# Banded attention and an MLP on one core: the scores of the third and fourth batches as 64 by 64 quarters of the TensorE array

## The chip, the core and the metric

The kernel runs on one core of one Trainium2 chip. The metric is device time in microseconds (us): the median of several runs of the whole program. One execution is also recorded by the hardware profiler; its instructions, waits and transfers are the profile that this document reads.

Engine names follow the profile: PE is TensorE's matmuls, PEld its weight loads, DVE is VectorE, ACT is ScalarE, POOL is GpSimd, SP is the engine whose queue issues all transfers. PSUM, into which PE writes, has eight banks.

## What is computed

Four batches of eight attention heads, each over 768 queries of 64 numbers, then for every batch a small mixing over tokens and a two-layer MLP. Cut to what matters here:

```python
B, H, S, D = 4, 8, 768, 64           # block = 32, window = 16, nb = 24
k_sum = k.reshape(B, H, nb, 32, D).max(axis=3)
v_sum = v.reshape(B, H, nb, 32, D).mean(axis=3)
scores_l = scale * q @ k.T            # kept where |i - j| < 16
scores_s = scale * q @ k_sum.T + log(32)
a = softmax(concat([scores_l, scores_s], axis=-1))
x = a @ concat([v, v_sum], axis=2)    # heads side by side: 768 x 512 per batch
u = x + (x.T @ U @ V).T
out = u + relu(u @ w_ch1) @ w_ch2     # 512 -> 2048 -> 512
```

## The kernel before

**Scores.** A head's 768 queries make six tiles of 128. A tile holds two groups of 64 queries, and each group sees its own 96 neighbouring keys and the 24 block maxima: 120 columns (`KC`). Both halves of the 128 partitions carry numbers of the 64 head dimensions: partitions 0 to 63 of the key tile `kt` hold the window of one group of 64 queries, partitions 64 to 127 that of the other. The query tile `qz` is laid out so that each group of 64 queries stands in its own half of the partitions, and zeros, written once at the start, stand in the other half. One matmul of 128 by 128 queries against 128 by 120 keys (line 321, `scores`) thus gives both groups their own keys: the zeros cancel the wrong half. Half of the array multiplies by zero. The work is in float32, and each such matmul shows in the trace as two weight loads and two matmuls (LDWEIGHTS and MATMUL). `scores(st, h, a)` does tiles 3a to 3a+2 into one PSUM bank, and `exponentials(st, h, a)` reads that bank: DVE adds the mask and takes the row's minimum (line 341), ACT takes the exponential (line 351).

**After the scores.** `turn_squares` (line 371) transposes blocks of 32 on DVE, a trip through memory (lines 376 and 384) turns the rest, `square_values` (line 423) multiplies with the values in 24 matmuls of 32 array columns each (`tile_position=(0, 32*i)`), and `normalise` (lines 435 to 437) divides. `mix_t` (line 537) and `mix_s` (line 555) begin the token mixing; `mix_rows` (line 601) and `operands` (lines 610, 184, 185, 636 to 648) finish it and make the operands of the MLP's first layer.

**The order of the work.** It is written by hand: each engine runs its instructions strictly in the order in which the program lists them. The first batch's attention runs alone. The attention of batches 2, 3 and 4 is cut into 32 steps per batch (`later_step`), with seven pieces of mixing put between them at a place that `MIX` sets and seven after them (`later_steps`), and these steps are spread between the matmuls of the MLP of the batch before (line 1185 onwards). For the third and fourth batches the first 15 steps (heads 0 to 4) fall in the MLP's first layer (line 1066, `up_phase`), the rest (heads 5 to 7 and the mixing) in its second (line 1151, `down_phase`). Step 3h does `scores(h, 0)` with its exponentials, step 3h+1 `scores(h, 1)` with its exponentials, step 3h+2 `square_values(h-2)`, `normalise(h-2)` and `turn_squares(h)`.

**Banks and weights.** All PSUM tiles share the eight banks. In `down_phase` six of them hold the accumulators `acc`, so that everything else takes turns in two. At the start of each of its 16 rounds (18 matmuls) `gates` has ACT (line 1135) and DVE (line 1136) make the left operands `gh` and `gl` of the next round. Weights come back from memory in `whole` (line 748), are rounded by ACT (line 184) and the rest taken by POOL (line 185).

Of the kernel before, what the change touches and what calls it, by code (L numbers as in the profile page):

```python
# [10 lines left out]
F32 = mybir.dt.float32  # L11
# [7 lines left out]
P = 128  # L19
BLOCK, WIN = 32, 16  # L20
NB = S // BLOCK
NU = S // P
W = 64 + 2 * WIN
KC = NB + W
# [4 lines left out]
ORDER = (1, 2, 3, 4, 5, 0)  # L29
KP = 2 * W + NB  # L30
# [54 lines left out]
def body(ctx: ExitStack, tc, q0, q1, k, v, vn, uv, w1, w2, mask, ident, rep, out):  # L85
    nc = tc.nc
# [4 lines left out]
    small = ctx.enter_context(tc.tile_pool(name="small", bufs=2))  # L91
# [5 lines left out]
    def bank(name):  # L97
        return psum.tile([P, 512], F32, name=name, tag="bank")
# [116 lines left out]
    def load_qk(st, h):  # L215
        load_k(st, h)
        load_q(st, h)
# [7 lines left out]
    def load_v(st, h):  # L225
        vt = kv.tile([KC, 2, NU, DV], F32, name="vt")
        nc.sync.dma_start(out=vt[:W, 0], in_=v[st.b, 0, :, h])
        nc.sync.dma_start(out=vt[NB:, 1], in_=v[st.b, 1, :, h])
        st.vt[h] = [vt[:, i] for i in range(2)]
# [7 lines left out]
    def load_vsum(st, g, i):  # L237

        parts = 1 if st.b == 0 else 2
        n = BLOCK * D // (2 * parts)  # L240
        spare = None
        if st.b == 1 or st.b == 2 and g == 0:
            spare = hidden_place(2 + i)
        st.vn[g, i] = []
        for j in range(parts):
            if st.b == 0:
                t = vn0[g, i]
            elif spare is not None:
                t = spare[:, j * n : (j + 1) * n]
            else:  # L250
                t = mo.tile([P, DM], F32, name="stage", tag="val", bufs=VALS)[:, :n]
            k = i * parts + j
            nc.sync.dma_start(out=t, in_=vn[st.b, g, :, k * n : (k + 1) * n])
            st.vn[g, i].append(t)
# [22 lines left out]
    def key_maxima(st, h):  # L277
        block_maxima(st, h)
        spread_maxima(st, h, nc.vector.tensor_copy)
# [25 lines left out]
    def value_summaries(st, h, i, copy):  # L305
        r0, r = 32 * (h % 4), (W, 0)[i]
        copy(
            st.vt[h][i][r : r + NB],
            st.vsum[h // 4][r0 : r0 + NB].unsqueeze(1).broadcast_to([NB, NU, DV]),
        )  # L310

    def scores(st, h, a):
        if h not in st.neg:
            st.neg[h] = small.tile([P, NU], F32, name="neg")
        qt, kt = st.qt[h].rearrange("p u q -> p (u q)"), st.kt[h]
        ps = bank("ps_s")
        for i in range(3):
            u = 3 * a + i
            j = ORDER.index(u)
            k0 = (j // 2) * KP + (j % 2) * KC  # L320
            nc.tensor.matmul(  # L321
                ps[:, i * KC : (i + 1) * KC],
                qt[:, 64 + j * P : 64 + j * P + P],
                kt[:, k0 : k0 + KC],
                start=True,
                stop=True,
            )
        st.ps_s[h, a] = ps

    def exponentials(st, h, a):  # L330
        ps = st.ps_s.pop((h, a))
        if h not in st.e and st.b == 0:
            st.e[h] = e0[h % 4]
        elif h not in st.e:
            st.e[h] = att.tile([P, NU * KC + PAD], F32, name="e", bufs=1)
            nc.gpsimd.memset(st.e[h][:, NU * KC :], 0.0)
        e = tiles_of(st.e[h])[:, 3 * a : 3 * a + 3]
        for i in range(3):
            u = 3 * a + i
            m = 0 if u == 0 else (3 if u == NU - 1 else 1 + u % 2)  # L340
            nc.vector.tensor_tensor_reduce(  # L341
                out=e[:, i, :],
                in0=ps[:, i * KC : (i + 1) * KC],
                in1=mask_sb[:, m, :],
                scale=-SCALE,
                scalar=BIG,
                op0=ALU.add,
                op1=ALU.min,
                accum_out=st.neg[h][:, u : u + 1],
            )  # L350
            nc.scalar.activation(  # L351
                e[:, i, :],
                e[:, i, :],
                AF.Exp,
                bias=st.neg[h][:, u : u + 1],
                scale=-1.0,
            )

    def tiles_of(e):
        return e[:, : NU * KC].rearrange("p (u k) -> p u k", k=KC)  # L360

    def turn_squares(st, h):

        e = st.e.pop(h)
        squares = att.tile([P, 4, NU, 32], F32, name="squares", bufs=1)

        src = bass.AP(tensor=e.tensor, offset=e.offset, ap=[e.ap[0], [32, 4], [KC, NU], [1, 32]])  # L370
        nc.vector.transpose(squares, src)
        st.at[h] = squares

    def send_squares(st, h):
        there = dram.tile([P, 4, NU * 32], F32, name="there")
        nc.sync.dma_start(out=there, in_=st.at[h].rearrange("p j u q -> p j (u q)"))
        st.at[h] = there

    def fetch_squares(st, h):

        there = st.at[h].rearrange("(i k) j c -> j k i c", k=32)
        at = st.at[h] = att.tile([P, 4, NU, 32], F32, name="at", bufs=1)
        for j in range(4):
            nc.sync.dma_start(
                out=at[32 * j : 32 * j + 32].rearrange("k i u q -> k i (u q)"), in_=there[j]
            )
# [30 lines left out]
    def square_values(st, h):  # L417

        at, vt = st.at.pop(h), st.vt[h]
        ps = st.psx[h] = bank("ps_x")  # L420
        for u in range(NU):
            for i in range(4):
                nc.tensor.matmul(  # L423
                    ps[32 * i : 32 * i + 32, u * DV : (u + 1) * DV],
                    at[:KC, i, u],
                    vt[u % 2][:, (u // 2) * 2 + (i // 2 + u) % 2],
                    start=True,
                    stop=True,
                    tile_position=(0, 32 * i),
                )  # L430

    def normalise(st, h):
        ps = st.psx.pop(h)[:, : NU * DV].rearrange("p (u d) -> p u d", d=DV)
        s = small.tile([P, NU], F32, name="sum")
        nc.vector.tensor_scalar_add(s, ps[:, :, D], 1e-9)
        nc.vector.reciprocal(s, s)
        nc.vector.tensor_tensor(
            st.x[:, :, h * D : (h + 1) * D],
            ps[:, :, :D],
            s.unsqueeze(2).broadcast_to([P, NU, D]),  # L440
            ALU.mult,
        )
# [25 lines left out]
            slow.pop(0)  # L468

    STEPS = 32  # L470
    MIX = (18, 30)

    def later_step(st, i):

        h, a = divmod(i, 3)
        if a == 0:
            if 1 <= h <= H:  # L480
                send_squares(st, h - 1)
            if 2 <= h <= H + 1:
                fetch_squares(st, h - 2)
            if h < H:
                scores(st, h, 0)
                exponentials(st, h, 0)
            if 3 <= h <= H:
                load_v(st, h - 1)
        elif a == 1:
            if h < H:  # L490
                scores(st, h, 1)
                exponentials(st, h, 1)
            if h + 1 < H:
                key_maxima(st, h + 1)
            if 1 <= h <= H:
                for t in range(2):
                    value_summaries(st, h - 1, t, nc.scalar.copy)
        else:
            if h + 2 < H:
                load_qk(st, h + 2)  # L500
            if h == 2:
                st.x = mo.tile([P, NU, DM], F32, name="x")
            if 2 <= h <= H + 1:
                square_values(st, h - 2)
                normalise(st, h - 2)
            if h < H:
                turn_squares(st, h)
        if st.b > 1:
            if i in (2, 5):
                load_vsum(st, 1, i // 5)  # L510
            if i in (4, 7):
                slow.append(add_vsum(st, 1, i // 7))
        if i in MIX:
            c = 2 * MIX.index(i)
            mix_t(st, c, 2)
            mix_t_out(st, c, 2)
        if i - 1 in MIX:
            c = 2 * MIX.index(i - 1)
            mix_s(st, c, 2)
            mix_s_out(st, c, 2)  # L520

    def later_steps(st):

        todo = [(later_step, st, i) for i in range(STEPS)]
        between = [(mix_rows, st, 0, k) for k in range(3)] + [(operands, st, 0, k) for k in range(4)]
        for n, x in enumerate(between):
            todo.insert(MIX[0] + 3 + 2 * n, x)
        return todo + [(mix_rows, st, 1, k) for k in range(3)] + [(operands, st, 1, k) for k in range(4)]


# [315 lines left out]
    st = sts[0]  # L846
# [98 lines left out]
    for word in START.split():  # L945
        name = word.rstrip("0123456789.")
# [238 lines left out]
    for b in range(1, B):  # L1185
        cur, ahead, after = ([*sts, None, None][b + i] for i in range(3))
        todo = later_steps(ahead) if ahead else []
# [120 lines left out]
```

## Time and profile before

| | |
|---|---|
| median of 3 runs | 678.85 us (678.16 to 680.5) |
| profiled execution | 678.02 us, of which the span of the profile is 676.2 us |
| granted TensorE clock | 0.995 of full speed |
| PE, PEld busy | 641.9 us, 568.2 us |
| DVE, ACT, POOL busy | 386.6, 343.1, 372.0 us |
| scores of batches 2 to 4 (line 321, `kt` and `qz`) | 288 matmul instructions, 39.7 us busy |
| third batch's attention steps | about 237 to 363 us |
| fourth batch's attention steps | about 392 to 519 us |

Busy shares alone don't tell what bounds the kernel. The chain of waits is followed back from the last instruction, from each to what released it. Matmuls overlap in the array: a row's duration includes the depth of the pipe, so what one costs is read from the distance between starts, or from its piece in the chain.

### The profile page before, as it was taken

What the parts mean: (1) busy time and instruction counts of PE and PEld (TensorE: products, weight loads), DVE (VectorE), ACT (ScalarE), POOL (GpSimd) and SP (SyncE); (2) the same over time, 40 slices, a digit from 0 to 9 for tenths busy, and PEclk for the clock granted to TensorE, in tenths of its full rate; (3) what the DMA queues carried; (4) which work ended last, traced back from release to release, by engine and by line L of the source; (5) the groups of instructions that cost most, each with busy time, mean ns of one, the idle gap of its engine ahead of it and who ended that gap; (6) DMA issues with size and microseconds to landing.
All of it is one profiled execution on the core that took longest, in us unless ns stands there. A gap on an engine that the chain in (4) does not pass through costs nothing.

```text
span 676.2 us, 13190 instructions
## 1 busy us (share of the span) xinstructions
PE 641.9 (95%) x4800; PEld 568.2 (84%) x4800; DVE 386.6 (57%) x1041; ACT 343.1 (51%) x751; POOL 372.0 (55%) x428
## 2 busy tenths in 40 slices
PE   5889997989999899999999999999999999999997
PEld 4768796879888799998877899998877899998886
DVE  3778798777898666555655634566654432232222
ACT  3855356355433556665453467665543365553322
POOL 5846967635697757651245486661334375563420
PEclk9999999899999999999999999999999999999999
DMA  9999679898992169785438059777432144431002
GB/s 250 249 345 279 218 231 297 252 272 305 279 330 100 52 185 309 209 250 151 143 104 248 23 174 311 229 222 220 127 97 79 55 148 165 139 126 62 32 0 94
DMA packets 82752, 124.47 MB, mean 184 GB/s; under 512 B 7680, under 2 KB 57728, under 8 KB 82688
## 3 DMA queue, kind: packets, MB, share of 16 engines
q1 hardware_dynamic: 82688, 123.63, 60.3%
q8 instruction: 38, 0.62, 0.4%
q14 instruction: 26, 0.21, 0.1%
HBM read 96.34 MB, written 27.26 MB: 183 GB/s over the span
## 4 chain that ended last, share of the span: by engine, by line
PE 75%; DMA 11%; DVE 6%; ACT 3%; SPq 2%; POOL 2%; issue 1%; ACTq 0%; POOLq 0%; DVEq 0%
PE acc L1151 27%; PE ps_h L1066 24%; PE acc L813 7%; PE ps_h L791 6%; PE ps_s L321 4%; PE ps_x L423 3%; DMA place<-in_q 2%; DMA qz<-in_q 2%; PE ps_o L610 2%; DMA place<-in_w 1%; DMA at<-there 1%; DMA place<-in_v 1%; DVE gl L1136 1%; DMA kt<-in_k 1%; DMA place<-in_k 1%
## 5 line engine op out<-in xcount | busy, mean ns | idle before, releaser
L185 POOL TENSOR_TENSOR parts<-whole,parts 128x512 fp32r<-128x512 f32 (+1 forms) x144 | 181.6, 1270 | 165.6 <-ACT parts L184 137.1
L1151 PE MATMUL acc<-parts,gh 128*128 128x512 f32 x576 | 193.4, 399 | 0.0
L1066 PE MATMUL ps_h<-op,parts 128*128 128x384 f32 x1008 | 188.4, 339 | 1.2 <-POOL parts L185 0.6
L1066 PEld LDWEIGHTS ps_h<-op,parts 128*128 128x128 f32 x1008 | 173.6, 188 | 3.1 <-POOL parts L185 0.9
L1151 PEld LDWEIGHTS acc<-parts,gh 128*128 128x128 f32 x576 | 108.1, 188 | 22.9 <-issue 0.8
L1151 PE MATMUL acc<-parts,gl 128*128 128x512 f32 x288 | 113.1, 393 | 1.9 <-DVE gl L1136 1.9
L1136 DVE SCALAR_TENSOR_TENSOR gl<-place,gh 128x768 fp32r<-128x768 f32 x48 | 58.9, 1228 | 83.1 <-ACT gh L1135 83.0
L184 ACT CAST parts<-whole 128x512 fp32r<-128x512 f32 (+1 forms) x144 | 83.5, 583 | 5.8 <-DMA whole<-up 4.3
L351 ACT ACTIVATE e<-e,neg 128x120 f32<-128x120 f32 x144 | 46.5, 386 | 59.7 <-DVE neg L341 53.6
L791 PE MATMUL ps_h<-place 128*128 128x384 f32 x384 | 74.3, 341 | 1.2 <-DVE place L592 0.5
L813 PE MATMUL acc<-place,gh 128*128 128x512 f32 x192 | 68.3, 411 | 2.1 <-POOL place L185 2.1
L791 PEld LDWEIGHTS ps_h<-place 128*128 128x128 f32 x384 | 66.6, 188 | 4.2 <-DVE place L592 1.3
L1135 ACT ACTIVATE gh<-place 128x768 fp32r<-128x768 f32 x48 | 40.6, 846 | 55.1 <-PE acc L1151 54.9
L1151 PEld LDWEIGHTS acc<-parts,gl 128*128 128x128 f32 x288 | 54.2, 188 | 13.1 <-DVE gl L1136 3.9
L160 POOL TENSOR_SCALAR val<-place 128x512 f32<-128x512 f32 (+1 forms) x30 | 48.7, 1638 | 29.6 <-ACT place L147 17.7
L185 POOL TENSOR_TENSOR place<-val,place 128x512 fp32r<-128x512 f32 x29 | 38.6, 1351 | 19.5 <-ACT place L184 19.5
L185 POOL TENSOR_TENSOR op<-tmp,op 128x384 fp32r<-128x384 f32 x24 | 24.5, 1030 | 42.7 <-ACT op L184 38.5
L341 DVE CUSTOM_DVE_ANT_0 e<-ps_s,mask_sb 128x120 f32<-128x120 f32 x144 | 32.9, 278 | 25.3 <-PE ps_s L321 24.5
L813 PEld LDWEIGHTS acc<-place,gh 128*128 128x128 f32 x192 | 36.6, 192 | 11.1 <-POOL place L185 3.4
L803 ACT ACTIVATE gh<-ps_h 128x384 fp32r<-128x384 f32 x32 | 15.6, 488 | 54.3 <-PE ps_h L791 54.1
L321 PEld LDWEIGHTS ps_s<-kt,qz 128*128 128x128 f32 x288 | 39.0, 191 | 4.4 <-DVE kt L303 1.6
L321 PE MATMUL ps_s<-kt,qz 128*128 128x120 f32 x288 | 39.7, 274 | 2.0 <-DVE kt L303 1.2
(110 smaller groups left out, 848.4 us busy)
## 6 DMA issues: line engine op xcount, KB each, us to landing
place<-in_w SPq DMA_DIRECT2D x32, 512.0 KB, 6.0
whole<-up SPq DMA_DIRECT2D x24, 512.0 KB, 4.0
whole<-down SPq DMA_DIRECT2D x24, 512.0 KB, 3.7
there<-squares SPq DMA_DIRECT2D x24, 384.0 KB, 4.2
at<-there SPq DMA_DIRECT2D x96, 96.0 KB, 3.9
whole<-up SPq DMA_DIRECT2D x24, 384.0 KB, 3.5
vt<-in_v SPq DMA_DIRECT2D x48, 146.2 KB, 4.0
kt<-in_k SPq DMA_DIRECT2D x24, 288.0 KB, 5.6
```

The source lines that it names most:

```text
L160: nc.gpsimd.tensor_scalar(f32(bits), f32(hi), 0.0, None, ALU.mult)
L184: nc.scalar.copy(hi, val)
L185: engine.tensor_tensor(lo, val, f32(hi), ALU.subtract)
L321: nc.tensor.matmul(ps[:, i * KC : (i + 1) * KC], qt[:, 64 + j * P : 64 + j * P + P], kt[:, k0 : k0 + KC], start=True, stop=True,)
L341: nc.vector.tensor_tensor_reduce(out=e[:, i, :], in0=ps[:, i * KC : (i + 1) * KC], in1=mask_sb[:, m, :], scale=-SCALE, scalar=BIG, op0=ALU ...
L351: nc.scalar.activation(e[:, i, :], e[:, i, :], AF.Exp, bias=st.neg[h][:, u : u + 1], scale=-1.0,)
L791: nc.tensor.matmul(ps[:, :NH], w_split[0, f][:, c % 2, part_w, c // 2], ut[:, c, :], start=(n == 0), stop=(n == 3 * NC - 1),)
L813: nc.tensor.matmul(acc[t], gt[:, sl], w_split[1, f][:, part_w], start=(first and j == 0), stop=(last and j == 2),)
L1066: nc.tensor.matmul(ps, a[:, sa, i], b[:, sb, i], start=(first and n == 0), stop=(n == 5), skip_group_check=not first,)
L1135: nc.scalar.activation(gh, h, AF.Relu)
L1136: nc.vector.scalar_tensor_tensor(gl, h, 0.0, f32(gh), ALU.max, ALU.subtract)
L1151: nc.tensor.matmul(acc[t], gt[:, sl], w[:, part_w], start=(f == 0 and j == 0), stop=(f == NF - 1 and j == 2),)
```

## The change

For the third and fourth batches (`st.b` of 2 and 3) the function `scores_by_subtiles` takes the place of the two calls of `scores`. It drops the zeros: a tile of 128 queries becomes two matmuls of 64 queries by 64 head dimensions against 120 keys, each on a quarter of the array (`tile_position=(r, c)`, r the row and c the column at which the quarter begins). It takes an even and an odd tile of queries together, so that four matmuls in a row use the four quarters; the even tile's results go to one bank, the odd tile's to another. All six tiles of a head are done at step 3h, 12 matmuls in all where there were 6; step 3h+1 keeps its exponentials. A bank now holds tiles 0, 2, 4 or 1, 3, 5 (`tiles_in_bank`). The first entry of `MIX` goes from 18 to 19 for these batches, which moves `mix_t` and `mix_s` of the first half, and the seven pieces between the steps, by one step. The zeros are still written and loaded.

```diff
+    def scores_by_subtiles(st, h):
+        st.neg[h] = small.tile([P, NU], F32, name="neg")
+        qt, kt = st.qt[h].rearrange("p u q -> p (u q)"), st.kt[h]
+        ps = [bank("ps_s") for _ in range(2)]
+        for i in range(3):
+            for s in range(2):
+                for a in range(2):
+                    j = ORDER.index(2 * i + a)
+                    q0, k0 = 64 + j * P + 64 * s, (j // 2) * KP + (j % 2) * KC
+                    r, c = 64 * ((s + a) % 2), 64 * s
+                    nc.tensor.matmul(
+                        ps[a][c : c + 64, i * KC : (i + 1) * KC],
+                        qt[r : r + 64, q0 : q0 + 64],
+                        kt[r : r + 64, k0 : k0 + KC],
+                        start=True,
+                        stop=True,
+                        tile_position=(r, c),
+                    )
+        for a in range(2):
+            st.ps_s[h, a] = ps[a]
+
+    def tiles_in_bank(st, a):
+        return [3 * a + i if st.b < 2 else 2 * i + a for i in range(3)]
...
-    MIX = (18, 30)
+    def mix_at(st):
+        return (18 if st.b < 2 else 19, 30)
...
             if h < H:
-                scores(st, h, 0)
+                if st.b < 2:
+                    scores(st, h, 0)
+                else:
+                    scores_by_subtiles(st, h)
                 exponentials(st, h, 0)
...
         elif a == 1:
             if h < H:
-                scores(st, h, 1)
+                if st.b < 2:
+                    scores(st, h, 1)
                 exponentials(st, h, 1)
...
-            todo.insert(MIX[0] + 3 + 2 * n, x)
+            todo.insert(mix_at(st)[0] + 3 + 2 * n, x)
```

Three places show how this moves instructions. `x6` and the like count instructions of one kind in a row; line numbers of the change are its own (344 is the new matmul, 369 the masked minimum that was 341, 1100 was 1066, 1170 was 1136).

PE in the first layer of the second batch's MLP, two heads of the third batch or the fourth, before:

```order
L321 MATMUL ps_s<-kt,qz_83 128x120 x3
L1066 MATMUL ps_h<-op,parts 128x384 x18
L423 MATMUL ps_x<-vt,at 32x65 x24
L1066 MATMUL ps_h<-op,parts 128x384 x24
L321 MATMUL ps_s<-kt,qz_84 128x120 x3
L1066 MATMUL ps_h<-op,parts 128x384 x18
L321 MATMUL ps_s<-kt,qz_84 128x120 x3
```

The same place now:

```order
L344 MATMUL ps_s<-kt,qz_83 64x120 x12
L1100 MATMUL ps_h<-op,parts 128x384 x36
L451 MATMUL ps_x<-vt,at 32x65 x24
L1100 MATMUL ps_h<-op,parts 128x384 x24
L344 MATMUL ps_s<-kt,qz_84 64x120 x12
```

Two groups of three whole matmuls have become one group of twelve quarter matmuls, at the place of the first of them.

DVE in the second layer, after the exponentials of head 6, before (`t_st` is the end of `mix_s`, `sum` to `x` are `normalise` of head 4, the third row from the end is `mix_rows`):

```order
L565 TENSOR_TENSOR t_st<-ps_r,t_st 64x256
L1136 SCALAR_TENSOR_TENSOR gl<-place,gh 128x768
L435 TENSOR_SCALAR sum<-ps_x 128x6
L436 RECIPROCAL sum<-sum 128x6
L437 TENSOR_TENSOR x<-ps_x,sum 128x6x64
L371 STREAM_TRANSPOSE squares<-e 128x768
L605 TENSOR_TENSOR x<-x,ps_u 128x2x256
L1136 SCALAR_TENSOR_TENSOR gl<-place,gh 128x768
L341 ISA e,neg<-ps_s,mask_sb 128x120
```

And now:

```order
L1170 SCALAR_TENSOR_TENSOR gl<-place,gh 128x768
L463 TENSOR_SCALAR sum<-ps_x 128x6
L464 RECIPROCAL sum<-sum 128x6
L465 TENSOR_TENSOR x<-ps_x,sum 128x6x64
L399 STREAM_TRANSPOSE squares<-e 128x768
L599 TENSOR_TENSOR t_st<-ps_r,t_st 64x256
L369 ISA e,neg<-ps_s,mask_sb 128x120
```

The last reads of `ps_x` and `ps_r` now stand right ahead of the first read of head 7's scores; `mix_rows`, which stood between, comes after them. On PE nine `acc` matmuls stand between `ps_r` and head 7's scores.

DVE later in the second layer, where `operands` (rows that read `ps_o`) meets `gl` of the next round, before:

```order
L1136 SCALAR_TENSOR_TENSOR gl<-place,gh 128x768
L185 TENSOR_TENSOR op<-ps_o,op 128x384
L636 TENSOR_TENSOR tmp<-ps_o,tmp 128x384
L1136 SCALAR_TENSOR_TENSOR gl<-place,gh 128x768
L185 TENSOR_TENSOR op<-ps_o,op 128x384
L641 TENSOR_TENSOR tmp<-tmp,ps_o 128x384
```

And now:

```order
L185 TENSOR_TENSOR op<-ps_o,op 128x384
L670 TENSOR_TENSOR tmp<-ps_o,tmp 128x384
L463 TENSOR_SCALAR sum<-ps_x 128x6
L464 RECIPROCAL sum<-sum 128x6
L465 TENSOR_TENSOR x<-ps_x,sum 128x6x64
L1170 SCALAR_TENSOR_TENSOR gl<-place,gh 128x768
```

`operands` has moved from just ahead of `gl` to earlier in a round, with `normalise` between them.

More of the change, by code (lines that the diff above doesn't have):

```diff
@@ L336, in exponentials @@
             nc.gpsimd.memset(st.e[h][:, NU * KC :], 0.0)
-        e = tiles_of(st.e[h])[:, 3 * a : 3 * a + 3]
-        for i in range(3):
-            u = 3 * a + i
+        e = tiles_of(st.e[h])
+        for i, u in enumerate(tiles_in_bank(st, a)):
             m = 0 if u == 0 else (3 if u == NU - 1 else 1 + u % 2)
             nc.vector.tensor_tensor_reduce(
-                out=e[:, i, :],
+                out=e[:, u, :],
                 in0=ps[:, i * KC : (i + 1) * KC],
@@ L351, in exponentials @@
             nc.scalar.activation(
-                e[:, i, :],
-                e[:, i, :],
+                e[:, u, :],
+                e[:, u, :],
                 AF.Exp,
@@ L512, in later_step @@
                 slow.append(add_vsum(st, 1, i // 7))
-        if i in MIX:
-            c = 2 * MIX.index(i)
+        if i in mix_at(st):
+            c = 2 * mix_at(st).index(i)
             mix_t(st, c, 2)
             mix_t_out(st, c, 2)
-        if i - 1 in MIX:
-            c = 2 * MIX.index(i - 1)
+        if i - 1 in mix_at(st):
+            c = 2 * mix_at(st).index(i - 1)
             mix_s(st, c, 2)
```

## The prediction

> **What bounds the kernel now.** I read the page first, then busy times by stage, then PE's waits in those stages, then the chain of waits in order of time, and the rows of the scores by shape.
>
> ```profile
> PE 641.9 (95%) x4800; PEld 568.2 (84%) x4800; DVE 386.6 (57%) x1041; ACT 343.1 (51%) x751; POOL 372.0 (55%) x428
> PE 75%; DMA 11%; DVE 6%; ACT 3%; SPq 2%; POOL 2%; issue 1%; ACTq 0%; POOLq 0%; DVEq 0%
> ```
>
> PE carries the chain. The stages that hold the third batch's attention are 232 to 300 us (first layer of the MLP) and 300 to 364 (second layer), and 386 to 456 and 456 to 520 for the fourth. The table gives the length, then each engine's busy time:
>
> ```profile
> 232.00:300.00 68.00, 66.16 (x531) 64.43 (x530) 42.92 (x140) 42.84 (x100) 44.02 (x56) 1.00 0.76 232
> 300.00:364.00 64.00, 63.05 (x563) 50.96 (x562) 36.04 (x92) 31.01 (x63) 22.19 (x20) 1.00 0.57 166
> 386.00:456.00 70.00, 69.39 (x555) 67.74 (x554) 36.68 (x133) 47.31 (x111) 49.03 (x65) 1.00 0.74 226
> 456.00:520.00 64.00, 63.07 (x561) 50.88 (x560) 35.64 (x92) 31.32 (x63) 22.14 (x20) 1.00 0.47 139
> 540.00:676.00 136.00, 131.54 (x682) 119.02 (x681) 38.14 (x54) 58.43 (x112) 60.54 (x49) 1.00 0.29 95
> ```
>
> PE idles 0.6 to 1.8 us in each of the four; DVE, ACT and POOL have a third or more of each free. The last row, behind all attention, is PE's as well. So PE time taken out of the four stages should reach the end, unless PE then waits for something that ran on its own clock. What PE waits for there now (total, times, longest), in the first layer at 230 to 300, at 386 to 455, and in either second layer:
>
> ```profile
> PE ps_h L1066 <- ACT place L1125: 0.5, 1, 0.5
> PE ps_h L1066 <- POOL parts L185: 0.6, 1, 0.6
> PE acc L1151 <- DVE gl L1136: 0.9, 2, 0.6
> ```
>
> **What a head's scores cost now.** Pieces of the chain in the second layer (start, length), where PE runs without a gap:
>
> ```profile
> 311.42 0.66 PE ps_s L321 x6
> 312.08 0.79 PE ps_m L537 x24
> 312.87 2.30 PE acc L1151 x9
> 315.17 0.66 PE ps_s L321 x6
> 315.83 0.44 PE ps_r L555 x2
> 316.27 2.07 PE acc L1151 x9
> 318.35 0.82 PE ps_x L423 x48
> 319.16 2.27 PE acc L1151 x9
> ...
> 323.77 0.66 PE ps_s L321 x6
> 324.43 2.09 PE acc L1151 x9
> ...
> 326.75 2.05 PE acc L1151 x9
> ```
>
> Three whole matmuls are six instructions: 0.66 us, 0.11 each. The nine `acc` behind them take 2.09 where the plainest nine take 2.05, so half a head costs 0.70 and a head 1.40. In the first layer the same:
>
> ```profile
> 267.17 0.66 PE ps_s L321 x6
> 267.83 3.16 PE ps_h L1066 x18
> 271.00 0.82 PE ps_x L423 x48
> 271.81 4.37 PE ps_h L1066 x24
> ```
>
> **What it will cost.** The trace before has no matmul on a quarter of the array, but it has two kinds on column strips, four at once (busy us, mean ns of one; the PEld row is the weight loads of its matmul):
>
> ```profile
> L321 PE MATMUL ps_s<-kt,qz 128*128 128x120 f32 x288 | 39.7, 274 | 2.0 <-DVE kt L303 1.2 <-DVE neg L341 0.8
> L423 PE MATMUL ps_x<-vt,at 120*32 120x65 f32 x1152 | 22.0, 225 | 5.0 <-DMA at<-there 3.8 <-DVE val L166 1.2
> L423 PEld LDWEIGHTS ps_x<-vt,at 120*32 120x32 f32 x1152 | 18.0, 112 | 12.6 <-issue 7.8 <-DVE val L166 1.6 <-DVE place L1092 0.7
> L537 PE MATMUL ps_m<-x,u_sb 128*32 128x128 f32 x192 | 7.5, 278 | 0.9 <-DVE gl L804 0.7 <-DVE x L437 0.3
> ```
>
> `mix_t` is the nearest row: 24 instructions on four strips, six on each, with 128 columns streamed. It costs 0.79 us, and the nine `acc` behind it take 2.30, 0.25 above plain: 1.04 in all. Six passes of 0.11 are 0.66, so going into strips and back costs about 0.38. `square_values` agrees: 48 instructions, 12 on each strip, 65 columns: 0.82 plus 0.22 behind it is 1.04 too; 12 passes of 65/120 of 0.11 are 0.72, which leaves 0.32. I take 0.35 for going in and out.
>
> A head in quarters is 12 matmuls, 24 instructions, 6 on each quarter, 120 columns. If all four quarters work at once, it costs 6 × 0.105 + 0.35 = 0.98, against 1.40. By the starts of the single instructions around these groups the whole form is a little cheaper (1.34) and the strip form too (about 1.00 for `mix_t`, 0.96 scaled to 120 columns); I take a saving of 0.38 a head. The change covers 2 batches of 8 heads: 16 × 0.38 = **6.1 us**. Bounds: with nothing to pay for going in and out, the saving would be 1.40 − 0.63 = 0.77 a head or 12.3 us, which both strip rows speak against; if row halves can't work at once, 12 passes, 12 × 0.105 + 0.35 = 1.61, a loss of 0.21 to 0.27 a head, 3.4 to 4.3 us. The strips of the trace all use the full height of the array, so no row here shows two matmuls at once on different rows; I choose the first value because what four strips share (issue, weight loads, PSUM writes) already runs four at once, each into its own partitions, and the even and odd tiles write to different banks.
>
> The Trainium skill bears on this. In "TensorE: Matmul & The Clock Gate", Part 3, a weight load overlaps matmuls in flight only when the row group differs; here the strips share all rows, and their loads do overlap: 12 loads of 112 ns mean per strip alone would be 1.3 us, and the whole of `square_values` took 0.82, so the trace disagrees. By that rule a quarter's next load would wait for its matmul, about 0.11 more in each of six passes, 1.6 a head: the price of the first rival below, to whose chance it adds nothing, since the trace speaks against it. The same section reports 3.07 times for four row tiles at once; by it the sum stays at 6.1. "TensorEngine Tiling (Array Packing)", Key Properties, says that changing the tiling mode drains the array; the 0.22 to 0.25 us behind the strip groups agree.
>
> **The other edits.** The masked minima and exponentials are the same instructions with other tiles; they lie on DVE and ACT under PE's matmuls. Those of step 3h+1 now find their scores ready, so DVE and ACT do them earlier. No transfer is added or moved in SP's queue, and query and key buffers come free a step earlier.
>
> Two banks at once matter in the second layer, where only two are spare. The tight place is head 7: PE does `ps_x`, `ps_r`, nine `acc` and then wants both banks, whose last readers are `normalise` (then the transpose) and `t_st`. Behind PE's wait stand the `acc` matmuls, hence everything. DVE for the head before, and `t_st`:
>
> ```profile
> 308.26 0.89 PE L423 MATMUL ps_x<-vt,at 120*32 120x65 f32 x48
> 309.21 0.17 DVE L435 TENSOR_SCALAR sum<-ps_x 128x6 f32<-128x6 f32 x1 [1.38 <-PE ps_x L423]
> 310.11 0.97 DVE L371 STREAM_TRANSPOSE squares<-e 128x768 f32<-128x768 f32 x1
> 311.00 0.92 DVE L1136 SCALAR_TENSOR_TENSOR gl<-place,gh 128x768 fp32r<-128x768 f32 x1
> 318.54 0.43 DVE L565 TENSOR_TENSOR t_st<-ps_r,t_st 64x256 fp32r<-64x256 f32 x1 [0.64 <-ACT t_st L563]
> ```
>
> From the start of `ps_x` DVE needs 0.95 to `sum`, 2.74 to the end of the transpose (311.00 − 308.26), 3.2 with `t_st`. PE comes after 0.82 + 0.44 + 2.07 = 3.33. It just fits; I put 0.25 us of wait for each batch, **0.5**; bounds nothing and the rival below.
>
> The wait for `gl` (0.9 in each second layer) comes where `operands` stands ahead of it on ACT and DVE. That piece moves earlier in its round, so I expect half of 1.8 us back, **0.9**; bounds 0 and 1.8. Against it, at about 259 PE waits 0.5 because the rounding of a weight block waited for its transfer:
>
> ```profile
> 250.48 5.37 DMA whole<-up
> 255.93 0.62 ACT parts L184
> ```
>
> PE will come there about 0.8 earlier (two heads), the transfer perhaps not: **0.5** lost, bounds 0 and 0.8.
>
> Sum: −6.1 + 0.5 − 0.9 + 0.5 = −6.0. From the profiled execution's 678.02 (span 676.2 and 1.8 around it) that gives 672.0; the median of the runs is 0.8 above it, so 678.85 − 6.0 = **672.9 us**.
>
> **Rivals.**
> *Only two quarters at once (slower).* Quarters in different rows exclude each other, in the array, in loading or in writing PSUM. Then each head pays 12 passes plus going in and out: 16 × 0.24 = 3.8 longer, with the other terms 682.8. It decides above 10 passes for a head: (1.38 − 0.35) / 0.105. For it: no row here shows row halves at once. Against it: nothing in the strips' rows shows a shared limit at four matmuls.
>
> *The pair of banks costs what the gap gives.* At 318.35 `sum` came late, behind a `gl` that waited for `gh`:
>
> ```profile
> 319.93 1.41 DVE L1136 SCALAR_TENSOR_TENSOR gl<-place,gh 128x768 fp32r<-128x768 f32 x1 [0.97 <-ACT gh L1135]
> 321.37 0.16 DVE L435 TENSOR_SCALAR sum<-ps_x 128x6 f32<-128x6 f32 x1
> ```
>
> With `sum` as late, at +3.0, DVE would be done with `t_st` at +5.3, and PE would wait 2 us, 4 in both batches: 676.9. Against it: ACT was late because exponentials, copies and `t_st` stood ahead of `gh`, and these now run earlier.
>
> *The first layer's gain is lost to the weights.* If transfers and POOL set the pace there, the gain of heads 0 to 4 goes, 10 × 0.38 = 3.8: 676.7. For it: the waits for POOL and ACT above. Against: they are short, and POOL is busy for 44 of 68 us and 49 of 70.
>
> **How the numbers follow.** Chances: forecast 0.72; two quarters at once 0.12; bank pair 0.08; weights 0.08. About 0.3%, 2.0 us, is what a measurement can tell from no change. The forecast's own range is 670.5 (all `gl` waits gone, 0.42 a head) to 674.5; to leave out no more than 2 in 10 it must reach to the cases near 677. Range 670.5 to 677.0. Faster: the forecast and most of the weights case with half of the bank case, 0.80; same 0.08; slower 0.12.
>
> **What would show it.** Right: in the chain a group of 24 `ps_s` at about 0.7 us, followed by nine `acc` at about 2.3; starts of four quarter matmuls within some 10 ns and a step of about 0.1 us to the next four. Wrong in the main step: a step of 0.2 us, or pieces of 1.2 us and more. Banks: PE waiting for DVE `t_st` or `x` ahead of head 7's scores. `gl`: its row among PE's waits shorter than 0.9. Weights: larger waits for `parts` or `place` in the first layer.

## The result

| | before | the change | second measurement |
|---|---|---|---|
| median, us | 678.62 (678.16 to 680.5, 4 runs) | 669.39 (667.98 to 672.54, 4 runs) | 669.45 against 677.99 |
| ratio to before, 95% interval | | 0.9864 (0.9831 to 0.9897) | 0.9881 (0.9852 to 0.9910) |
| profiled execution, us (its span) | 678.02 (676.2) | 668.83 (667.0) | span 665.5 |

The change is faster, by 9.2 us in the first measurement and 8.5 in the second. The forecast was 672.9 with a range of 670.5 to 677.0: right in sign, but the time is 3.5 us below the forecast and outside the range.

**Where the time went.** I cut both executions at the starts of the MLP's layers. First the stages before, as the windows of the trace give them (length, then busy time of PE, PEld, DVE, ACT, POOL with the number of instructions, then granted clock, DMA share, GB/s):

```profile
0.00:230.67 230.67, 205.36 (x1709) 179.19 (x1709) 172.82 (x498) 115.98 (x274) 156.18 (x202) 0.99 0.83 250
230.67:300.55 69.88, 68.03 (x543) 66.31 (x542) 44.77 (x143) 43.44 (x101) 44.57 (x56) 1.00 0.75 227
300.55:386.40 85.85, 84.90 (x665) 68.93 (x665) 49.07 (x114) 39.62 (x79) 33.81 (x35) 1.00 0.49 145
386.40:456.16 69.76, 69.14 (x554) 67.57 (x553) 36.44 (x132) 46.91 (x110) 48.79 (x65) 1.00 0.75 227
456.16:542.10 85.94, 85.01 (x665) 68.91 (x665) 47.22 (x108) 39.68 (x79) 29.77 (x27) 1.00 0.39 114
542.10:676.20 134.10, 129.44 (x673) 117.30 (x671) 36.29 (x51) 57.42 (x110) 58.90 (x47) 1.00 0.30 97
```

The same stages with the change:

```profile
0.00:229.91 229.91, 205.61 (x1708) 179.08 (x1709) 172.41 (x498) 115.88 (x274) 156.12 (x202) 0.99 0.84 251
229.91:298.57 68.66, 66.16 (x604) 62.39 (x603) 43.26 (x143) 43.32 (x101) 44.60 (x56) 1.00 0.75 231
298.57:381.89 83.32, 83.32 (x702) 66.57 (x701) 47.31 (x114) 39.93 (x79) 33.10 (x35) 1.00 0.51 150
381.89:449.37 67.48, 67.19 (x614) 63.59 (x613) 38.77 (x132) 46.32 (x110) 48.87 (x65) 1.00 0.77 234
449.37:532.89 83.52, 83.33 (x701) 66.57 (x701) 45.49 (x108) 39.92 (x79) 29.09 (x27) 1.00 0.39 117
532.89:667.00 134.11, 129.44 (x673) 117.32 (x671) 36.30 (x51) 57.23 (x110) 58.91 (x47) 0.99 0.30 97
```

The two first layers (second and fourth row) are 1.2 and 2.3 us shorter, the two second layers 2.5 and 2.4. The last stage is the same to 0.01 us: what was won ahead of it was kept. In the third batch's second layer PE is now busy without a gap, 83.32 of 83.32 us; in the fourth batch's it idles 0.2 us of 83.52, ahead of head 3's `square_values`. The first stage holds no changed instruction, and yet is 0.8 us shorter; more on that below. On the page of the change PE has fewer busy microseconds with more instructions, and still carries the chain:

```profile
PE 635.0 (95%) x4992; PEld 555.5 (83%) x4992; DVE 383.5 (57%) x1041; ACT 342.6 (51%) x751; POOL 370.7 (56%) x428
PE 72%; DMA 12%; POOL 7%; DVE 3%; issue 2%; ACT 2%; SPq 1%; ACTq 0%; POOLq 0%; DVEq 0%
```

**What a head costs now.** Pieces of the chain in the second layer of the change, whose first two rows are head 5, then `square_values`, then head 6:

```profile
299.43 0.78 PE ps_s L344 x24
300.20 0.89 PE acc L1185 x3
...
305.97 0.87 PE ps_x L451 x48
306.84 2.26 PE acc L1185 x9
309.10 0.78 PE ps_s L344 x24
309.88 2.26 PE acc L1185 x9
```

24 instructions take 0.78 us and the nine `acc` behind them 2.26, 0.21 above the plain 2.05: 0.99 a head. The forecast said 0.98, and that a group would show about 0.7 and 2.3. The trace's single starts show the four quarters at work together (us, a head of the first layer):

```
249.541 249.548 249.554 249.561 | 249.694 249.701 249.708 249.714 | 249.797 249.803 249.810 249.817
249.899 249.906 249.913 249.919 | 250.002 250.008 250.015 250.022 | 250.104 250.111 250.118 250.124
```

Four start within 20 ns; the next four come 0.153 us after the first ones, and from then on every four 0.102 us after the last. From the last whole matmul ahead to the second one behind, less two plain steps, a head costs 0.98 us now and 1.34 before in the first layer, 0.99 and 1.36 in the second. That is 0.36 or 0.37 a head, 16 × 0.36 = 5.8 us; the forecast had 6.1.

**What PE waits for.** In the first layers of the change, at 230 to 300 and 386 to 455:

```profile
PE ps_h L1100 <- ACT place L1159: 1.2, 1, 1.2
PE ps_h L1100 <- POOL parts L185: 0.3, 1, 0.3
```

The wait for ACT has grown from 0.5 to 1.2, the one for POOL has shrunk from 0.6 to 0.3. In the second layers the wait for `gl`, 0.9 in each before, has no row any more. Its worth is larger than its row: before, four steps between `acc` matmuls around the two waits were 1.004, 0.337, 0.720 and 0.335 us where a plain step is 0.229, 1.48 us too much. The row counts only from the modelled end of the matmul ahead, some 0.4 us after its start, and leaves out the slow second step. The weight loads' row for the same two waits errs the other way:

```profile
PEld acc L1151 <- DVE gl L1136: 1.8, 2, 1.0
```

The account of the two profiles: scores −5.8, `gl` −3.0 (2 × 1.48), ACT's wait +0.7, POOL's −0.3, first stage −0.8, in all −9.2, which is the difference of the spans, 676.2 − 667.0.

### The profile page after: what moved, and what is told of

It is laid out like the page before. It is cut to its first block, busy times and chain, and to the rows that moved or that the text cites. A ratio compares the mean times of both kernels' runs of the same rounds, so it can differ in the third digit from the quotient of the medians.

```text
span 667.0 us, 13598 instructions
## 1 busy us (share of the span) xinstructions
PE 635.0 (95%) x4992; PEld 555.5 (83%) x4992; DVE 383.5 (57%) x1041; ACT 342.6 (51%) x751; POOL 370.7 (56%) x428
## 4 chain that ended last, share of the span: by engine, by line
PE 72%; DMA 12%; POOL 7%; DVE 3%; issue 2%; ACT 2%; SPq 1%; ACTq 0%; POOLq 0%; DVEq 0%
PE acc L1185 30%; PE ps_h L1100 24%; PE acc L847 6%; PE ps_h L825 4%; DMA place<-in_k 3%; PE ps_x L451 3%; DMA place<-in_vn 2%; PE ps_o L644 2%; POOL val L160 2%; PE ps_s L344 2%; DMA place<-in_w 1%; DMA at<-there 1%; POOL place L185 1%; POOL place L261 1%; DMA kt<-in_k 1%
## 5 line engine op out<-in xcount | busy, mean ns | idle before, releaser
L1100 PE MATMUL ps_h<-op,parts 128*128 128x384 f32 x1008 | 186.0, 338 | 1.5 <-ACT place L1159 1.2
L1170 DVE SCALAR_TENSOR_TENSOR gl<-place,gh 128x768 fp32r<-128x768 f32 x48 | 56.3, 1173 | 97.1 <-ACT gh L1169 97.1
L847 PE MATMUL acc<-place,gl 128*128 128x512 f32 x96 | 38.3, 399 | 0.0
L1160 DVE TENSOR_TENSOR place<-place,ps_h 128x384 f32<-128x384 f32 x24 | 13.3, 553 | 37.0 <-ACT place L1159 37.0
```

The lines of the kernel that those rows point to most:

```text
L847: nc.tensor.matmul(acc[t], gt[:, sl], w_split[1, f][:, part_w], start=(first and j == 0), stop=(last and j == 2),)
L1100: nc.tensor.matmul(ps, a[:, sa, i], b[:, sb, i], start=(first and n == 0), stop=(n == 5), skip_group_check=not first,)
L1170: nc.vector.scalar_tensor_tensor(gl, h, 0.0, f32(gh), ALU.max, ALU.subtract)
```

## The experiments

Each diff is against the change's kernel; only the lines that matter are shown.

### Which part gives what: the mixing alone, the quarters alone

The first keeps whole scores in two banks at two steps, and moves the mixing by one step as the change does:

```diff
-                if st.b < 2:
-                    scores(st, h, 0)
-                else:
-                    scores_by_subtiles(st, h)
+                scores(st, h, 0)
...
-        return [3 * a + i if st.b < 2 else 2 * i + a for i in range(3)]
+        return [3 * a + i for i in range(3)]
```

(`scores(st, h, 1)` likewise.) Expected:

> The scores stay whole (as before), only the token mixing and the pieces between the steps move by one step for the third and fourth batches. Theory: the waits of PE for gl in the two second layers come from operands standing just ahead of gl; moving it takes them away, 1.48 us of PE starts in each second layer, so 3.0 us: about 675.6 us (ratio 0.9956), no row of PE waiting for DVE gl, and first layers as before. Rival: gl comes in time because both tiles' scores are ready at once and DVE and ACT run ahead; then the waits stay at 0.9 in each second layer and the time at 678.6.

The second keeps the quarters and leaves the mixing where it was:

```diff
-        return (18 if st.b < 2 else 19, 30)
+        return (18, 30)
```

Expected:

> The scores in quarters, the mixing where it was before. Theory: 16 heads by 0.36 us are won and the waits for gl come back (1.48 in each second layer); the start of the mixing at head 6 now wants a third bank beside the two of the scores and waits for three masked minima, about 0.6 us in each batch: 678.6 - 5.8 + 0.4 + 1.2 = 674.4 us (ratio 0.994). Rival (the early scores free gl): no wait for gl, about 671 us.

Measured: the mixing alone 675.77 us, ratio 0.9955 (0.9933 to 0.9976), where 0.9956 was expected; the quarters alone 673.87, ratio 0.9918 (0.9896 to 0.9940), where 0.994 was expected. The second layers with the mixing alone:

```profile
301.66:386.18 84.52, 84.52 (x666) 69.07 (x665) 47.59 (x114) 40.12 (x79) 33.14 (x35) 1.00 0.50 147
455.84:540.40 84.56, 84.56 (x665) 69.07 (x665) 45.73 (x108) 40.12 (x79) 29.11 (x27) 1.00 0.39 116
```

They are 1.3 and 1.4 us shorter than before with the old scores, and PE has no gap: no row of PE waiting for `gl` is left. So the move of the mixing frees `gl`, and the rival (early scores) falls. What PE waits for in the second layer with the quarters alone:

```profile
PE acc L1185 <- DVE gl L1170: 0.9, 2, 0.6
PE ps_m L571 <- DVE neg L369: 0.9, 1, 0.9
```

The wait for `gl` is back, word for word, and there is a new one: `mix_t` stands right behind the two banks of scores and must wait until three masked minima have emptied one (0.9, expected 0.6). Both second layers show it in their lengths:

| stage, us | before | mixing alone | quarters alone | the change |
|---|---|---|---|---|
| second layer, third batch | 85.85 | 84.52 | 85.65 | 83.32 |
| second layer, fourth batch | 85.94 | 84.56 | 85.87 | 83.52 |
| first layer, fourth batch | 69.76 | 69.67 | 67.47 | 67.48 |

In a second layer the quarters win almost nothing alone: 3 × 0.37 = 1.1 less, 0.9 for the bank. With the mixing moved both come together: 2.5 us. The move of the mixing is not a mere by-product: it is worth about 1.4 by itself and 0.9 more as the quarters' condition.

### Is it four at once, or are quarters cheap?

The same twelve matmuls in another order. First all of one column half, an even and an odd tile in turn:

```diff
-        for i in range(3):
-            for s in range(2):
+        for s in range(2):
+            for i in range(3):
                 for a in range(2):
```

> The change, with the twelve matmuls of a head in another order: first all of one column half, an even and an odd tile in turn, then the other column half, so that two quarters in different rows work at once and not four. Theory (what pays is four at once, one pass of about 0.102 us): 12 passes, 1.06 us from the first to the last start where it was 0.58; 16 by 0.48 is 7.7 us longer, 677 us. Rival (a quarter is cheap by itself, in loading and streaming): 0.58 and 669.4 as with the change. Rival (row halves exclude each other): about 2.1 and 693.

Then quarter by quarter:

```diff
-        for i in range(3):
-            for s in range(2):
-                for a in range(2):
+        for s in range(2):
+            for a in range(2):
+                for i in range(3):
```

> The change, with the twelve matmuls of a head quarter by quarter, three in a row on each, so that two on different quarters meet only where one quarter follows another. Theory: four times five steps of 0.102 us, 2.1 us from the first to the last start; 16 by 1.5 is 24 us longer, 693 us. Rival (a quarter is cheap by itself): as with the change, 0.58 and 669.4.

Measured, one execution each: 670.99 and 679.55 us, where theory said 677 and 693 and the rival 669.4. The matmul rows of the change, of the first and of the second order (busy us, mean ns of one):

```profile
L344 PE MATMUL ps_s<-kt,qz 64*64 64x120 f32 x384 | 13.5, 271 | 0.0
```

```profile
L344 PE MATMUL ps_s<-kt,qz 64*64 64x120 f32 x384 | 17.6, 271 | 0.0
```

```profile
L344 PE MATMUL ps_s<-kt,qz 64*64 64x120 f32 x384 | 25.8, 271 | 0.0
```

The mean duration, whose end is modelled, is 271 ns in all three; what differs is how many are at work at once. From the first to the last start a head takes 0.583, 0.839 and 1.348 us. That is 0.26 and 0.77 us a head more than the change, 4.1 and 12.2 us for 16 heads. The time of the first order's one execution, only 1.6 us over the change's median, doesn't show it by itself: its first stage was 1.8 us shorter than in the change's profile (228.13 against 229.91), by chance, while its second layers were 0.8 and 0.7 us longer. The rival (a quarter is cheap by itself) falls: quarter by quarter a head costs 0.98 + 0.77 = 1.75 us, more than the 1.34 of the whole form. That row halves exclude each other falls too: in the first order two quarters of one column half and different rows start 7 ns apart. But the theory's sizes, 1.06 and 2.1, were wrong too: only half of the added time came. The starts show why. Quarter by quarter (first layer, us):

```
263.449 263.603 263.705 263.711 263.808 263.864 263.910 263.967 263.973 264.013 264.069 264.126
264.172 264.228 264.234 264.274 264.331 264.388 264.433 264.490 264.536 264.593 264.695 264.798
```

A first quarter's six instructions come 0.10 to 0.15 apart, and another series sets in at 263.711, another at 263.973 and another at 264.234, 0.262 us apart, each while the one before it still has three instructions to start. (The trace shows which start opens a series: these four last 313 ns, the other twenty 262 or 263.) So PE did not keep the program's order of starts, though it is said ahead of the prediction that each engine does: it began the next quarter's instructions ahead of those that still stood before them, over a short distance. Mostly two series overlap that way. In the change's own order all four do. I had worked the sizes out as if nothing could overtake; that PE's reach is three instructions of a quarter is a reading of these starts, not tested apart.

### What going in and out costs

`square_values` (strips) put right ahead of the scores (quarters) at four places, heads 0 and 1 of both batches, one step later than before:

```diff
+            if st.b >= 2 and h in (3, 4):
+                square_values(st, h - 3)
+                scores_by_subtiles(st, h)
+                normalise(st, h - 3)
             if 2 <= h <= H + 1:
                 fetch_squares(st, h - 2)
...
```

(At their old places these three calls are left out for these heads.)

> The change, but heads 0 and 1 of the third and fourth batches do their square_values right ahead of the scores of heads 3 and 4, with no whole matmul between: four places where quarters follow strips. Theory (going between the whole array and pieces of it costs 0.35 us, between kinds of pieces nothing): from the last whole matmul to the second whole one behind, a place costs 0.63 + 0.67 + 0.35 over the plain steps instead of two times 0.35, so 4 by 0.35 is 1.4 us shorter, 668.0 us. Rival (any change of the shape of the pieces costs the same): as with the change, 669.4.

Measured: 668.18 us in one execution, too close to 669.4 to tell apart by itself. The chain at the first of the places:

```profile
273.80 0.82 PE ps_x L451 x48
274.62 0.78 PE ps_s L344 x24
275.40 10.66 PE ps_h L1106 x60
```

The change has there, as two places:

```profile
270.56 4.37 PE ps_h L1100 x24
274.93 0.78 PE ps_s L344 x24
275.71 6.47 PE ps_h L1100 x36
282.18 0.82 PE ps_x L451 x48
```

Side by side the pieces sum to 12.26 us, apart to 12.44: 0.18 less; by single starts 0.20. Theory said 0.35. From the last strip to the first quarter 0.150 us pass, as from the last strip to a whole matmul. So going from strips to quarters isn't free either: a bit over half of the price is saved. The fourth batch's first layer, which holds two of the places, took 67.12 us where the change's took 67.48, so both show in full; four such places are worth 0.7 to 0.8 us. In this profile PE also waited 0.3 for `at` ahead of head 3's `square_values` in the fourth batch. That is not the edit's doing, though the expectation of the last run (below) counts a later fetch for it: the edit makes the fetches of heads 1 and 2 later, the profile with only the later transfers has the same wait at the same place, and the profile of both edits has none.

### The second batch too

`scores_by_subtiles` and the later mixing from `st.b` of 1 on:

```diff
-                if st.b < 2:
+                if st.b < 1:
```

(so in all four places that the change made depend on the batch.)

> The change for the second batch too, whose attention runs under the first batch's MLP, where six banks are accumulators and the layer's own ps_h shares the other two with the attention. Theory (two banks at once are the price): 8 by 0.36 is 2.9 us won, but PE waits for ACT or DVE to free a bank in about half of the heads or more, 0.5 to 1.5 us each: 669.4 - 2.9 + 4 = 670.5 us, with new rows of PE waiting for DVE or ACT ahead of ps_s and ps_h between 80 and 170 us. Rival (banks are free in time, as in the later batches): 666.5 us.

Measured: 679.41 us, ratio to before 1.0018 (0.9993 to 1.0043). The direction was right, the price some two and a half times what was expected: the second batch's first layer began at 237.13 us where the change's began at 229.91, 7.2 later though 2.9 should have been won, 10.1 in all in place of 4. (In the other profiles that start varies by up to 4 us.) What PE waits for at 72 to 237 us:

```profile
PE ps_s L344 <- DVE gl L838: 6.6, 4, 2.3
PE acc L847 <- POOL place L185: 3.1, 3, 2.0
PE ps_h L825 <- DVE neg L369: 3.0, 3, 1.2
PE ps_h L825 <- ACT e L379: 1.6, 1, 1.6
```

Before, the first and the last of these rows aren't there, `place` stands at 2.1, and the third is small:

```profile
PE ps_h L791 <- DVE neg L341: 0.3, 1, 0.3
```

With the layer's own `ps_h` in one of the two spare banks, the pair waits for `gl`, which reads `ps_h`, and the next `ps_h` waits for the minima that empty the pair. In the second layers under which heads 5 to 7 of the third and fourth batches run, the layer's own `ps_h` is done after the first 6 us and leaves the two spare banks to them. There and in the first layers the same edit wins 5.8 us; here it loses all that the change wins in the whole kernel.

### What is left in the first layer

PE's wait (`ps_h` for ACT, 1.2 us in the second batch's first layer) followed a weight block's transfer (`whole`). The transfers of the second group of values, and the additions that use them, one step later:

```diff
-            if i in (2, 5):
-                load_vsum(st, 1, i // 5)
-            if i in (4, 7):
-                slow.append(add_vsum(st, 1, i // 7))
+            if i in (3, 6):
+                load_vsum(st, 1, i // 6)
+            if i in (5, 8):
+                slow.append(add_vsum(st, 1, i // 8))
```

> The change, with the transfers of the values' second group (and the additions that use them) one step later, so that a weight block in SP's queue goes ahead of them. Theory (PE's wait for ACT in the first layer of the second batch's MLP, 1.2 us with the change and 2.1 and 2.7 in the two halves of it, is this weight block's transfer, which stands behind those transfers): the wait is gone or below 0.5, 1 to 2 us shorter, about 668.0 us. Rival (the block is late because its buffer comes free late or all transfers are slow): the wait stays at 1 us or more, 669.4.

Measured: 669.49 us, ratio to before 0.9864 (0.9827 to 0.9901), no difference from the change that these runs could show. In its profile the wait is gone: PE's waits between 225 and 303 us have no row for ACT, and that layer takes 67.50 us as the fourth batch's does (67.48), where the change took 68.65 and 69.63 in its two profiles. So the cause is shown, and its worth, 1.2 to 2.1 us in a profile, is below what these runs can tell. In two profiles the wait cost more than itself: behind the 2.7 us of the quarters alone and the 2.5 of the run with the second batch's quarters the granted clock was 0.50 for about 3 us, ten matmuls in a row of 384 columns started 0.320 us apart where a plain step is 0.174, and some 1.5 us more were lost. Behind the waits of 2.1 and 2.2 us (the mixing alone, the change's second profile) no such steps show.

### The change again, and the last two edits together

The change itself was run once more. Expected:

> The change as it is, a second time. By the account of the two profiles the scores give 5.8 us and gl 3.0, the wait in the second batch's first layer and the first 230 us, which the change does not touch, vary by 1 to 2 us from one execution to the next. Theory (these two are chance): 8.0 to 9.0 us faster than before on the median, ratio 0.987 to 0.988, and the first layer of the second batch's MLP begins somewhere between 228 and 232 us. Rival (the first 0.8 us belong to the change): it begins at 230 us or earlier, and the ratio is 0.986 again.

Measured: ratio 0.9881 (0.9852 to 0.9910), at the upper end of what theory gave, though the interval holds the rival's 0.986 too, and the second batch's first layer began at 227.68 us, just ahead of the window that theory gave (228 to 232) and early, as the rival had it. So this run alone does not settle it; the other profiles do. Ahead of that point nothing differs between these kernels (but for the one with the second batch's quarters). In the ten profiles of the others, before, the change twice and seven experiments, it began between 227.7 and 231.6 us, and the latest of them, 231.63, is the change with the later transfers. The 0.8 us that the change's profile had ahead there are chance. The granted clock differed as well: from 110 us to the end of this stage it was 0.97 before and in the change's first profile, and 1.00 in the second, whose stage was 2.2 us shorter. How much of the spread that makes is open. Its wait for ACT was 2.2 us this time; in the profiles without the later transfers it was between 0.5 and 2.7, whatever the scores.

Strips beside quarters and the later transfers together:

> The change with strips and quarters side by side at four places and the value transfers a step later. By the profiles of the two alone, four times 0.20 us less, 0.5 back for a later fetch, and 1.2 for the wait: 1.5 us shorter than the change, ratio 0.998 to it, which is below what the rounds can tell; the profile is to show no wait for ACT in the second batch's first layer.

Measured: 666.77 us, ratio to before 0.9845 (0.9814 to 0.9876); no wait for ACT in the second batch's first layer, as expected. It is faster than before without doubt, and 2.7 us below the change in the same measurement, but the two intervals overlap, so that it beats the change is likely and not shown.

## Why the prediction was right or wrong

- **The scores: right.** 0.98 a head was forecast and 0.98 to 0.99 measured, 5.8 us in place of 6.1; the whole form costs 1.34 to 1.36 by its starts, not the 1.40 of the chain's pieces. Nearest row (`mix_t`, as many instructions on as many columns) and the price of 0.35 for going in and out held. Row halves work at once, which no row before had shown (7 ns between the starts of two quarters in different rows). The Trainium skill's rule in "TensorE: Matmul & The Clock Gate", Part 3, that a load overlaps matmuls in flight only when the row group differs, doesn't hold here either: the next loads of all four quarters started 0.053 us after the first matmuls, each on its own matmul's rows, and where the order is quarter by quarter and no other quarter was yet at work, 0.054 us after.
- **The wait for `gl`: mis-sized, the step that failed.** The prediction read 0.9 us in each second layer from PE's waits, took half of it and set the bound at 1.8 for both. It measured 1.48 a layer by the starts, and 1.3 to 1.4 when taken away alone, and all of it went. The profiles differ by 9.2 us where 6.0 was forecast; of the 3.2 between, about 2 lie here, 2.7 to 3.0 in place of 0.9; 0.8 are the first stage's chance, 0.5 the banks and 0.3 POOL's wait, and the scores and ACT's wait take 0.5 off again. The mechanism was right (`operands` stands ahead of `gl`), the quantity was not: an idle row counts from a modelled end, and a stalled stream of matmuls loses more than that. The row of the weight loads, 1.8 a layer, stood in the same trace and would have been the upper bound.
- **The two banks: no cost.** 0.5 us was put down; PE never waited. At head 7 of the third batch DVE ended `t_st` 0.12 us ahead of PE:

```profile
318.13 0.43 DVE L599 TENSOR_TENSOR t_st<-ps_r,t_st 64x256 fp32r<-64x256 f32 x1
```

  318.56 against the start of the scores at 318.68. "It just fits" was right. The rival on the banks had the right mechanism at another place: with the mixing unmoved it is `mix_t` that waits.
- **The weights: near, by luck.** 0.5 us more wait was forecast because PE comes there earlier, and 0.7 came (1.2 after 0.5). But the change's second profile shows 2.2, and the mixing alone, whose first layer keeps the old scores, 2.1. The wait varies from execution to execution, and no run shows that it grew with the earlier scores. The rival by which the weights eat the first layers' gain fell: these are 1.2 and 2.3 us shorter. (In the fourth batch's first layer POOL had 30% of its time free and ACT 32%, a little less than the third that was read there; nothing hung on it.)
- **The slower rival** (two quarters at once) fell with the starts.
- **The range** was too narrow because the unknown terms were bounded by idle rows, and because its lower end left no room for chance: it is about what remains with 1.8 us of `gl` rows gone, 0.42 a head, and nothing for banks and weights, while the first 230 us alone varied by 4 us between profiles of the same instructions.

## What to carry to other kernels

Small matmuls that fill a quarter of the array are worth packing four at once, in an order that goes round the quarters, and going in and out of that form has a price (0.35 us here, against 0.1 us for each pass of four) which the saved passes have to earn back. A packed form wants its results in several banks at once: look at who reads the banks' last contents, since an edit that moves the neighbours by one step can decide the gain. Size a stall by the distances between starts of the stalled stream, not by its idle row. A term that varies by itself from execution to execution can't be checked on one pair of profiles.

## What the hardware showed

- Starts of matmuls on quarters of the array don't keep the program's order: with three matmuls in a row on each quarter, the next quarter's series began 0.262 us after the one before, when that one still had three of six instructions to start.
- Four 64 by 64 matmuls in float32 on four quarters start within 20 ns and repeat every 0.102 us with 120 columns (0.153 for the first repeat). A quarter's own instructions keep the same distances when only one or two quarters are at work.
- Going from strips (32 columns) straight to quarters costs about 0.15 us, worked out as the 0.35 of leaving strips for the whole array and the whole array for quarters, less the 0.20 saved.
- After PE had waited 2.5 and 2.7 us, its granted clock was 0.50 for about 3 us, and a matmul of 384 columns took 0.320 us from start to start in place of 0.174; after 2.1 and 2.2 us it was not.
